# An attention and feed-forward kernel: head pairs taken two at a time on TensorE, PSUM pools laid out anew behind the opening, and the order of every engine written out

## The chip, the cores and the metric

The kernel runs on one core of a Trainium2 chip. Five engines work beside each other, each through its own instructions in order: TensorE (PE in the profile; PEld is its weight load), VectorE (DVE), ScalarE (ACT), GpSimd (POOL) and SyncE (SP), whose queue issues all loads and stores here. The metric is the device time of one execution in microseconds; lower is better.

## The reference

Queries, keys and values have 4 batches x 8 heads x 768 positions x 64. Each query sees the keys less than 16 positions away, and 24 summaries of blocks of 32 keys (the maximum of the keys, the mean of the values, with log 32 added to the score). The result is laid side by side by heads (512 columns) and goes through a feed-forward layer with 2048 hidden columns.

```python
k_sum = k.reshape(B, H, nb, block, D).max(axis=3)      # block 32
v_sum = v.reshape(B, H, nb, block, D).mean(axis=3)
scores_l = where(|i - j| < 16, scale * q @ k.T, -1e9)
scores_s = scale * q @ k_sum.T + log(block)
a = softmax(concatenate([scores_l, scores_s]))         # + 1e-9 under the fraction
x = a @ concatenate([v, v_sum])                        # heads side by side: 3072 x 512
h = x @ w_in
g = where(h >= 1, h, where(h <= -1, 0, (h + 1) ** 2 / 4))
out = g @ w_out
```

## The kernel before

The 3072 tokens are cut into eight chunks of 384 (half a batch each). A chunk's attention runs over four pairs of heads; a pair's two heads (j = 0, 1) lie in the two halves of the partitions. 384 queries are six blocks of 64, and each block sees a window of 96 keys and the 24 summaries: 120 columns.

Every step has a letter, and behind it the chunk, then the pair, hidden tile or part. For a pair: k, q, v load (k[c,p] is the windows, 360 KB; q 384 KB, half of it zeros, since the two heads' queries stand in their own columns of a block of 128), and r, y load the raw keys and values at the first chunk of a batch; R takes the maxima of the keys and C spreads them behind the windows; S makes the scores (12 matmuls in float32, L247, which the profile counts as 24); M masks them and takes the row maxima; E, D, N are the exponentials, the reciprocals of their sums and the product of both; t turns the result with 12 transposes of 32x32 blocks on VectorE (L300; T and P do so on TensorE and ScalarE in chunks 0 and 1); Y, z and x make the value means and spread them behind the windows of values; A multiplies with the values (again 12 matmuls, counted as 24, L310); X and L split the result into a high and a low part (xhi, xlo).

The feed-forward part goes through 16 hidden tiles of 128 per chunk. F (L331) is the first layer: four parts of three matmuls into one PSUM bank h, of which there are two (the pool ps_h). G and H (ACT), I (DVE, the last to read h; L350), J (ACT) and O (POOL, L360) make the activation and split it. B (L369) is the second layer: nine matmuls into the three banks acc of the chunk, two hidden tiles behind F (LAG = 2). U copies acc out and o stores it.

PSUM has the two banks of ps_h and six of the pool ps, which scores, turned weights, values and acc share. Up to the first F steps of chunk 1 the order of every engine is written out (OPENING, under tc.manual_schedule()). From there on the program lists, for each hidden tile, F, G, H, I, J, O, then one quarter of a pair's attention of the next chunk (a generator, attention), then B; Tile's scheduler orders each engine's instructions from that by its own costs. One pair therefore takes four hidden tiles, and TensorE makes eight short visits a chunk between F and B: four of scores, four of values.

The softmax weights of a pair lie in one tile e of two buffers, the turned weights in one tile turned_blocks for both heads of a pair. Raw keys, raw values and outputs share three buffers (tag "w" of the pool stage); keys, values and queries have two each.

## Time and profile before

| | |
|---|---|
| time, median of three runs | 666.75 us (664.21 to 668.29) |
| the profiled execution | 664.14 us |
| its span, first to last instruction | 662.4 us |
| granted TensorE clock, mean | 0.992 |
| TensorE busy | 638.6 us, 96% |
| VectorE, ScalarE, GpSimd busy | 57%, 53%, 45% |
| DMA | 69.07 MB, mean 104 GB/s |

The profile shows one execution. A busy time sums what an engine executed; matmuls overlap, and their ends are modelled. In the timeline a row has the start, the duration, the engine, the line, the operation, what it writes and reads, its shape and how often; in brackets the idle time before it and what released the engine. Neighbours of one kind are merged into one row (x24). In a row of stages stand the stage, its length, busy time and count of PE, PEld, DVE, ACT and POOL (or of those that match), the granted clock, the DMA share and GB/s. Times in the trace count from its first instruction.

### The profile page before, as it was taken

To read this page: it belongs to the slowest core of one execution; us is meant where nothing else is said; L and a number is where in the kernel's file an instruction comes from. 1 tells how busy PE (TensorE), PEld (TensorE's weight loads), DVE (VectorE), ACT (ScalarE), POOL (GpSimd) and SP (SyncE) were. 2 spreads that over 40 slices of the span, in tenths; PEclk is the share of its full clock that TensorE was granted. 3 is DMA by queue.
4 is the path that set the end of the run, shared out by engine and by line. 5 is a ranking of instruction groups with operands and counts; after the bars stand their busy time and mean duration, and the time that the engine had idled before them with its cause. 6 is when DMAs were issued, how large, how long until landed. Compare 5 with 4: busy or idle time off the path is not lost.

```text
span 662.4 us, 11908 instructions
## 1 busy us (share of the span) xinstructions
PE 638.6 (96%) x4442; PEld 559.9 (85%) x4442; DVE 376.8 (57%) x897; ACT 348.7 (53%) x881; POOL 295.2 (45%) x296
## 2 busy tenths in 40 slices
PE   8789997879999999999899999999999999999997
PEld 8679896758888888888788888888888888889996
DVE  5999974668445745557554755449645654431111
ACT  3899965644544454544544554554444545444332
POOL 2669985544444444225444433425444334222221
PEclk9999999898999999999999999999999999999999
DMA  8999502842222412145211411127102210001001
GB/s 293 325 355 332 216 1 103 284 156 65 66 65 65 135 44 66 46 133 186 66 52 32 160 50 62 64 81 239 56 29 65 99 60 19 2 1 47 1 0 48
DMA packets 31401, 69.07 MB, mean 104 GB/s; under 512 B 2928, under 2 KB 11376, under 8 KB 31344
## 3 DMA queue, kind: packets, MB, share of 16 engines
...
q14 instruction: 22, 0.18, 0.1%
...
## 4 chain that ended last, share of the span: by engine, by line
PE 78%; DVE 10%; DMA 5%; ACT 3%; issue 2%; POOL 1%; SPq 0%; POOLq 0%; DVEq 0%; ACTq 0%
PE acc L369 37%; PE h L331 35%; PE o_ps L310 3%; PE s_ps L247 3%; DMA first<-in_kT 2%; ACT e L267 2%; DVE turned_blocks L300 1%; DMA vraw<-in_vT 1%; DVE e L257 1%; DVE t L350 1%; DVE den L262 1%; DVE c L124 1%; DVE den L272 1%; DVE sums L213 1%; POOL e L277 1%
## 5 line engine op out<-in xcount | busy, mean ns | idle before, releaser
L331 PE MATMUL h<-xhi,halves 128*128 128x384 f32 x1024 | 284.8, 340 | 2.0 <-DVE t L350 2.0
L360 POOL TENSOR_TENSOR glo<-t,ghi 128x384 fp32r<-128x384 f32 x128 | 129.7, 1015 | 279.0 <-ACT ghi L355 185.7
L369 PE MATMUL acc<-halves,ghi 128*128 128x512 f32 x768 | 240.7, 394 | 0.0
L331 PEld LDWEIGHTS h<-xhi,halves 128*128 128x128 f32 x1024 | 188.5, 189 | 8.5 <-issue 2.1
L350 DVE SCALAR_TENSOR_TENSOR t<-h,t 128x384 f32<-128x384 f32 x128 | 70.9, 556 | 187.0 <-ACT t L347 178.6
L331 PE MATMUL h<-xlo,halves 128*128 128x384 f32 x512 | 173.9, 340 | 0.0
L369 PEld LDWEIGHTS acc<-halves,ghi 128*128 128x128 f32 x768 | 144.7, 188 | 28.8
L369 PE MATMUL acc<-halves,glo 128*128 128x512 f32 x384 | 156.7, 408 | 1.5 <-POOL glo L360 1.5
L355 ACT CAST ghi<-t 128x384 fp32r<-128x384 f32 x128 | 65.4, 513 | 150.0 <-DVE t L350 149.9
L344 ACT ACTIVATE t<-h,ones_half 128x384 f32<-128x384 f32 x128 | 73.7, 576 | 107.2 <-PE h L331 105.5
L300 DVE STREAM_TRANSPOSE turned_blocks<-e 32x192 f32<-32x192 f32 x288 | 106.5, 370 | 30.1 <-POOL e L277 25.7
L331 PEld LDWEIGHTS h<-xlo,halves 128*128 128x128 f32 x512 | 96.6, 189 | 5.7 <-DVE xlo L321 0.2
L267 ACT ACTIVATE e<-e,den 128x120 f32<-128x120 f32 x192 | 73.3, 383 | 28.3 <-DVE den L262 28.2
L369 PEld LDWEIGHTS acc<-halves,glo 128*128 128x128 f32 x384 | 72.1, 188 | 18.5 <-issue 3.6
L347 ACT ACTIVATE t<-t 128x384 f32<-128x384 f32 x128 | 67.1, 525 | 4.0
L277 POOL TENSOR_TENSOR e<-e,den 128x360 f32<-128x360 f32 x64 | 50.4, 790 | 40.6 <-DVE den L273 22.7
L222 POOL TENSOR_SCALAR v<-means 32x768 f32<-32x768 f32 x24 | 51.1, 2128 | 5.1 <-DVE means L219 1.6
L143 POOL TENSOR_TENSOR halves<-w,halves 128x1024 fp32r<-128x1024 f32 x16 | 38.5, 2417 | 3.4 <-ACT halves L137 2.8
L272 DVE TENSOR_SCALAR den<-den 128x3 f32<-128x3 f32 x64 | 16.4, 257 | 35.5 <-ACT e L267 35.4
L267 ACT ACTIVATION_READ_ACCUMULATOR e<-e,den 128x1 f32 x192 | 35.9, 187 | 0.0
L257 DVE SCALAR_TENSOR_TENSOR e<-s_ps,mask_sb 128x360 f32<-128x360 f32 x64 | 30.8, 523 | 1.8 <-PE s_ps L247 1.8
L262 DVE TENSOR_REDUCE den<-e 128x3 f32<-128x360 f32 x64 | 30.5, 518 | 0.0
...
## 6 DMA issues: line engine op xcount, KB each, us to landing
q<-in_q SPq DMA_DIRECT2D x30, 384.0 KB, 4.2
...
raw<-in_w_in SPq DMA_DIRECT2D x16, 512.0 KB, 10.5
raw<-in_w_out SPq DMA_DIRECT2D x16, 512.0 KB, 10.7
...
kraw<-in_kT SPq DMA_DIRECT2D x13, 384.0 KB, 4.0
vraw<-in_vT SPq DMA_DIRECT2D x13, 384.0 KB, 4.0
```

What stands on the lines that cost most here:

```text
L143: nc.gpsimd.tensor_tensor(out=lo, in0=converting[i].bitcast(F32), in1=hi.bitcast(F32), op=ALU.subtract)
L222: nc.gpsimd.tensor_scalar(out=v_ts[c, p][KW:], in0=means[p * SB:(p + 1) * SB].unsqueeze(1).broadcast_to([SB, NB, P]), scalar1=1.0 / SB, sc ...
L267: nc.scalar.activation(out=e[:, t, :], in_=e[:, t, :], func=AF.Exp, bias=nm[:, t:t + 1], scale=1.0, accum_out=den[:, t:t + 1])
L277: nc.gpsimd.tensor_tensor(out=e, in0=e, in1=den.unsqueeze(2).broadcast_to([P, NT, KA]), op=ALU.mult)
L300: nc.vector.transpose(out=pt[kb * SB:(kb + 1) * SB, :, qb * SB:(qb + 1) * SB], in_=e[qb * SB:(qb + 1) * SB, :, at:at + SB])
L331: nc.tensor.matmul(hs[c, f][:, :T], weight["win", f][w][:, k * P:(k + 1) * P], x, start=(k == 0 and n == 0), stop=(k == NK - 1 and n == 2))
L344: nc.scalar.activation(out=ts[c, f], in_=hs[c, f][:, :T], func=AF.Relu, bias=ones_half, scale=0.5)
L347: nc.scalar.square(out=ts[c, f], in_=ts[c, f])
L350: nc.vector.scalar_tensor_tensor(out=ts[c, f], in0=hs[c, f][:, :T], scalar=1.0, in1=ts[c, f], op0=ALU.max, op1=ALU.min)
L355: nc.scalar.copy(out=hi, in_=ts[c, f])
L360: nc.gpsimd.tensor_tensor(out=lo, in0=ts[c, f], in1=hi.bitcast(F32), op=ALU.subtract)
L369: nc.tensor.matmul(acc[c][i], a[:, rows], weight["wout", f][w], start=(f == 0 and n == 0), stop=(f == NF - 1 and n == 2))
```

## The change

It leaves the opening's order and the arithmetic as they are, with these edits behind and around it:

- Steps s and p take the scores and the values of two pairs (h = 0 or 1) in one go: 24 matmuls, counted as 48. The four banks for s are one of ps_h and three of a new pool ps_att, which p shares; acc has a new pool ps_acc of three banks. Both, and a new att_later, are opened where ps and att are closed behind the opening.
- Masks (n) are single steps; maxima (i), reciprocals (h) and products (l) take both heads of a pair in one instruction; each exponential (g) and each row of transposes (t) is a step. e holds two pairs in one buffer, turned_blocks two pairs.
- The value means are scaled on VectorE (u) ahead of their transposes, and x is a copy instead of a product.
- From chunk 1 on queries are loaded without zeros, by two DMAs of half the partitions; chunk 0's first two pairs of queries go to a room of the weights, as the other two did.
- SECOND (the feed-forward part of chunk 1) and LATER (chunks 2 to 7, and the end) write out the order of everything behind the opening. A sign stands for the chunk: "." the chunk whose feed-forward part runs, "-" the one before, "+" the next and "*" the one after that. Steps that were done are skipped.

In this diff a line of "..." stands where lines are left out.

```diff
 """
+SECOND = """
+v+0 v+1 F.00 F.01 F.02 F.03 r+0 k+0 q+0 r+1 G.0 k+1 q+1 H.0 I.0 R+0 J.0 F.10 F.11 F.12 F.13 O.0 R+1 C+0 G.1 C+1 y+0
+y+1 H.1 I.1 J.1 F.20 F.21 F.22 F.23 U-1 O.1 o-1 u+0 s+0 G.2 H.2 u+1 U-0 k+2 U-2 o-0 n+00 B.0 o-2 I.2 q+2 n+01 J.2 n+10
+k+3 n+11 q+3 i+0 F.30 F.31 F.32 F.33 O.2 i+1 r+2 g+00 r+3 g+01 z+0 g+02 z+1 B.1 G.3 x+0 g+03 x+1 H.3 g+04 I.3 g+05
+F.40 F.41 F.42 F.43 R+2 J.3 g+10 O.3 h+0 g+11 R+3 g+12 l+0 g+13 B.2 y+2 G.4 y+3 g+14 C+2 t+00 H.4 C+3 g+15 t+01 F.50
+F.51 F.52 F.53 I.4 h+1 J.4 l+1 t+02 B.3 G.5 O.4 t+03 H.5 I.5 J.5 F.60 F.61 F.62 F.63 t+10 O.5 t+11 B.4 G.6 t+12 H.6
+t+13 I.6 J.6 F.70 F.71 F.72 F.73 u+2 O.6 u+3 p+0 G.7 H.7 z+2 I.7 X+0 v+2 B.5 X+1 v+3 z+3 J.7 L+0 L+1 F.80 F.81 F.82
+F.83 O.7 x+2 B.6 G.8 x+3 H.8 I.8 J.8 F.90 F.91 F.92 F.93 O.8 s+1 G.9 H.9 I.9 r*0 B.7 n+20 J.9 k*0 n+21 q*0 n+30 n+31
+r*1 i+2 F.a0 F.a1 F.a2 F.a3 O.9 k*1 q*1 i+3 g+20 g+21 R*0 g+22 B.8 G.a C*0 g+23 H.a R*1 g+24 g+25 I.a C*1 y*0 F.b0
+F.b1 F.b2 F.b3 g+30 h+2 y*1 J.a l+2 g+31 g+32 g+33 B.9 O.a t+20 G.b g+34 t+21 H.b g+35 I.b F.c0 F.c1 F.c2 F.c3 h+3 J.b
+l+3 t+22 t+23 B.a G.c O.b H.c t+30 I.c t+31 F.d0 F.d1 F.d2 F.d3 J.c O.c t+32 t+33 B.b G.d H.d u*0 F.e0 F.e1 F.e2 F.e3
+I.d z*0 J.d u*1 O.d p+1 G.e H.e z*1 I.e X+2 v*0 B.c X+3 v*1 L+2 J.e L+3 F.f0 F.f1 F.f2 F.f3 O.e x*0 B.d G.f x*1 H.f
+I.f J.f
+"""
+LATER = """
+F.00 F.01 F.02 F.03 O-f s+0 G.0 H.0 I.0 k+2 B-e n+00 J.0 q+2 n+01 n+10 k+3 n+11 q+3 i+0 F.10 F.11 F.12 F.13 O.0 i+1
+g+00 g+01 g+02 B-f G.1 g+03 H.1 g+04 I.1 g+05 F.20 F.21 F.22 F.23 U-1 U-0 h+0 U-2 o-1 l+0 J.1 o-0 g+10 o-2 g+11 B.0
+G.2 O.1 t+00 g+12 t+01 H.2 r+2 g+13 r+3 F.30 F.31 F.32 F.33 I.2 g+14 g+15 t+02 J.2 h+1 O.2 t+03 B.1 G.3 l+1 H.3 R+2
+I.3 F.40 F.41 F.42 F.43 C+2 t+10 J.3 t+11 O.3 B.2 G.4 t+12 H.4 t+13 I.4 J.4 F.50 F.51 F.52 F.53 O.4 R+3 C+3 y+2 B.3
+G.5 y+3 H.5 I.5 J.5 F.60 F.61 F.62 F.63 O.5 u+2 p+0 G.6 u+3 H.6 I.6 X+0 v+2 B.4 z+2 X+1 v+3 J.6 L+0 L+1 z+3 F.70 F.71
+F.72 F.73 O.6 x+2 B.5 G.7 x+3 H.7 I.7 J.7 F.80 F.81 F.82 F.83 O.7 s+1 G.8 H.8 I.8 r*0 B.6 n+20 J.8 k*0 n+21 q*0 n+30
+n+31 r*1 i+2 F.90 F.91 F.92 F.93 O.8 k*1 q*1 i+3 g+20 g+21 R*0 g+22 B.7 G.9 C*0 g+23 H.9 R*1 g+24 g+25 I.9 C*1 y*0
+F.a0 F.a1 F.a2 F.a3 g+30 h+2 y*1 J.9 l+2 g+31 g+32 g+33 B.8 O.9 t+20 G.a g+34 t+21 H.a g+35 I.a F.b0 F.b1 F.b2 F.b3
+h+3 J.a l+3 t+22 t+23 B.9 G.b O.a H.b t+30 I.b t+31 F.c0 F.c1 F.c2 F.c3 J.b O.b t+32 t+33 B.a G.c H.c u*0 F.d0 F.d1
+F.d2 F.d3 I.c z*0 J.c u*1 O.c B.b G.d H.d z*1 I.d F.e0 F.e1 F.e2 F.e3 J.d O.d p+1 G.e H.e I.e X+2 v*0 B.c X+3 v*1 L+2
+J.e L+3 F.f0 F.f1 F.f2 F.f3 O.e x*0 B.d G.f x*1 H.f I.f J.f
+"""
 FIRST = [[("k", 2), ("q", 2)], [("k", 3), ("q", 3)], [("kraw", 1), ("vraw", 1)], [("kraw", 2), ("vraw", 2)],
-         [("kraw", 3), ("vraw", 3)], [("v", 2), ("v", 3)]]
+         [("kraw", 3), ("vraw", 3)], [("v", 2), ("v", 3)],
+         [("q", 0), ("q", 1)]]
 K_COPY = "vgvg"
 HI_POOL = [0, 2, 4, 6, 8, 10, 12, 14]
 
...
     load = ctx.enter_context(tc.tile_pool(name="load", bufs=2))
     ps_h = ctx.enter_context(tc.tile_pool(name="ps_h", bufs=2, space=PSUM))
-    ps = ctx.enter_context(tc.tile_pool(name="ps", bufs=6, space=PSUM))
+    opening = ExitStack()
+    ps = opening.enter_context(tc.tile_pool(name="ps", bufs=6, space=PSUM))
+    att = opening.enter_context(tc.tile_pool(name="att", bufs=2))
...
     def load_queries(c, p):
         b, hf = divmod(c, NHALF)
-        q_ts[c, p] = input_tile(load, "q", [P, NB, P], c, p)
-        nc.sync.dma_start(out=q_ts[c, p], in_=q2[b, p, :, hf * NB:(hf + 1) * NB, :])
+        blocks = slice(hf * NB, (hf + 1) * NB)
+        q_ts[c, p] = input_tile(load, "q", [P, NB, QB], c, p)
+        if c == 0:
+            nc.sync.dma_start(out=q_ts[c, p], in_=q2[b, p, :, blocks, :])
+        else:
+            for j in range(2):
+                rows = slice(j * D, (j + 1) * D)
+                nc.sync.dma_start(out=q_ts[c, p][rows], in_=q2[b, p, rows, blocks, rows])
...
+    def sum_vals_ahead(c, p):
+        part = sums[:, p, SB - NSUM:]
+        nc.vector.tensor_reduce(out=part, in_=raws["v", p].rearrange("p (n j) -> p n j", j=SB), axis=AX.X, op=ALU.add)
+        nc.vector.tensor_scalar_mul(out=part, in0=part, scalar1=1.0 / SB)
...
     def spread_sums(c, p):
-        nc.gpsimd.tensor_scalar(out=v_ts[c, p][KW:], in0=means[p * SB:(p + 1) * SB].unsqueeze(1).broadcast_to([SB, NB, P]),
-                                scalar1=1.0 / SB, scalar2=None, op0=ALU.mult)
+        nc.gpsimd.tensor_copy(out=v_ts[c, p][KW:], in_=means[p * SB:(p + 1) * SB].unsqueeze(1).broadcast_to([SB, NB, P]))
...
+    def scores_of_two(c, h):
+        for n in range(2 * NT):
+            b, t = divmod(n, NT)
+            p = 2 * h + b
+            if t == 0:
+                for j in range(2):
+                    where, tag = (ps_h, "h") if (b, j) == (0, 0) else (ps_att, "att")
+                    s_pss[c, p, j] = where.tile([P, 512], F32, tag=tag, name=f"s_ps{c}_{p}_{j}")
+            q_t, k_t = q_ts[c, p], k_ts[c, p]
+            for j in range(2):
+                rows = slice(j * D, (j + 1) * D)
+                for i in range(2):
+                    nc.tensor.matmul(s_pss[c, p, j][i * QB:(i + 1) * QB, t * KA:(t + 1) * KA], q_t[rows, 2 * t + i],
+                                     k_t[rows, 2 * t + i], start=True, stop=True)
+    def mask_of(c, p, j):
+        h, b = divmod(p, 2)
+        if (c, h) not in es:
+            es[c, h] = att.tile([P, 2, 2, NT, KA], F32, tag="e", name=f"e{c}_{h}", bufs=1)
+        at = c % NHALF
+        nc.vector.scalar_tensor_tensor(
+            out=es[c, h][:, b, j], in0=s_pss[c, p, j][:, :NT * KA].rearrange("p (t n) -> p t n", n=KA), scalar=1.0 / math.sqrt(D),
+            in1=mask_sb[:, at:at + NT], op0=ALU.mult, op1=ALU.add)
+    def maxima(c, p):
+        h, b = divmod(p, 2)
+        dens[c, p] = att.tile([P, 2, 2, NT], F32, tag=f"den{b}", name=f"den{c}_{p}")
+        nc.vector.tensor_reduce(out=dens[c, p][:, 0].rearrange("p j t -> p (j t)"), in_=es[c, h][:, b].rearrange("p j t k -> p (j t) k"), axis=AX.X, op=ALU.max, negate=True)
+    def exp_of(c, p, u):
+        h, b = divmod(p, 2)
+        j, t = divmod(u, NT)
+        e = es[c, h][:, b, j, t, :]
+        nc.scalar.activation(out=e, in_=e, func=AF.Exp, bias=dens[c, p][:, 0, j, t:t + 1], scale=1.0,
+                             accum_out=dens[c, p][:, 1, j, t:t + 1])
+    def reciprocals_of_pair(c, p):
+        den = dens[c, p][:, 1].rearrange("p j t -> p (j t)")
+        nc.vector.tensor_scalar_add(out=den, in0=den, scalar1=1e-9)
+        nc.vector.reciprocal(out=den, in_=den)
+    def norms_of_pair(c, p):
+        h, b = divmod(p, 2)
+        e = es[c, h][:, b].rearrange("p j t k -> p (j t) k")
+        den = dens[c, p][:, 1].rearrange("p j t -> p (j t)")
+        nc.gpsimd.tensor_tensor(out=e, in0=e, in1=den.unsqueeze(2).broadcast_to([P, 2 * NT, KA]), op=ALU.mult)
+    def turn_blocks(c, p, kb):
+        h, b = divmod(p, 2)
+        e = es[c, h][:, b].rearrange("p j t k -> p (j t) k")
+        pt = turned_blocks[:, b]
+        at = min(kb * SB, KA - SB)
+        for qb in range(P // SB):
+            if kb == P // SB - 1 or kb - qb % 2 in (0, 1):
+                nc.vector.transpose(out=pt[kb * SB:(kb + 1) * SB, :, qb * SB:(qb + 1) * SB],
+                                    in_=e[qb * SB:(qb + 1) * SB, :, at:at + SB])
+    def values_of_two(c, h):
+        for b in range(2):
+            p = 2 * h + b
+            o_pss[c, p] = ps_att.tile([P, 512], F32, tag="att", name=f"o_ps{c}_{p}")
+            for blk in range(NB):
+                t, i = divmod(blk, 2)
+                for j in range(2):
+                    nc.tensor.matmul(o_pss[c, p][j * D:(j + 1) * D, blk * QB:(blk + 1) * QB], v_ts[c, p][:, blk, j * D:(j + 1) * D],
+                                     turned_blocks[:, b, j * NT + t, i * QB:(i + 1) * QB], start=True, stop=True)
...
-            acc[c] = [ps.tile([P, DM], F32, tag="ps", name=f"acc{c}_{i}") for i in range(NTT)]
+            acc[c] = [(ps if c == 0 else ps_acc).tile([P, DM], F32, tag="ps", name=f"acc{c}_{i}") for i in range(NTT)]
...
+    def at_chunk(text, c):
+        for step in text.split():
+            at = c + "-.+*".index(step[1]) - 1
+            if at < NCH and not (step[0] in "rRyuz" and at % NHALF):
+                do(step[0] + str(at) + step[2:])
...
     with tc.manual_schedule():
         do(OPENING)
-    turned_on_vector.update(range(NHALF, NCH))
-    turned_blocks = att.tile([P, 2, T], F32, tag="pt", name="turned_blocks", bufs=1)
-    for j in range(2):
-        nc.gpsimd.memset(turned_blocks[:, j], 0.0)
-    sums = const.tile([P, NPAIR, SB], F32, name="sums")
-    means = const.tile([P, P], F32, name="means")
-    nc.gpsimd.memset(sums, 0.0)
-
-    ahead = {c: attention(c) for c in range(1, NCH)}
-    for i in range(NF, NCH * NF + LAG):
-        c, f = divmod(i, NF)
-        if i < NCH * NF:
-            s = f"{c}{f:x}"
-            do(f"F{s}0 F{s}1 F{s}2 F{s}3 G{s} H{s} I{s} J{s} O{s}")
-            if c + 1 < NCH:
-                next(ahead[c + 1])
-        c, f = divmod(i - LAG, NF)
-        do(f"B{c}{f:x}")
-        if f == NF - 1:
-            do(" ".join(f"U{c}{i} o{c}{i}" for i in range(NTT)))
+        opening.close()
+        att = ctx.enter_context(tc.tile_pool(name="att_later", bufs=2))
+        ps_acc = ctx.enter_context(tc.tile_pool(name="ps_acc", bufs=NTT, space=PSUM))
+        ps_att = ctx.enter_context(tc.tile_pool(name="ps_att", bufs=3, space=PSUM))
+        turned_blocks = att.tile([P, 2, 2 * NT, P], F32, tag="turned", name="turned_blocks", bufs=1)
+        for b in range(2):
+            nc.gpsimd.memset(turned_blocks[:, b], 0.0)
+        sums = const.tile([P, NPAIR, SB], F32, name="sums")
+        means = const.tile([P, P], F32, name="means")
+        nc.gpsimd.memset(sums, 0.0)
+        at_chunk(SECOND, 1)
+        for c in range(2, NCH + 1):
+            at_chunk(LATER, c)
```

More of the change, by code (lines that the diff above doesn't have):

```diff
@@ L218, in turn_sums @@
             rows = slice(a * SB, (a + 1) * SB)
-            nc.vector.transpose(out=means[p * SB:(p + 1) * SB, rows], in_=sums[rows, p, :])
+            nc.vector.transpose(out=means[p * SB:(p + 1) * SB, rows], in_=sums[rows, p])
     def spread_sums(c, p):
-        nc.gpsimd.tensor_scalar(out=v_ts[c, p][KW:], in0=means[p * SB:(p + 1) * SB].unsqueeze(1).broadcast_to([SB, NB, P]),
-                                scalar1=1.0 / SB, scalar2=None, op0=ALU.mult)
+        nc.gpsimd.tensor_copy(out=v_ts[c, p][KW:], in_=means[p * SB:(p + 1) * SB].unsqueeze(1).broadcast_to([SB, NB, P]))
     def turn_vals(c, p):
@@ L247, in scores @@
                     nc.tensor.matmul(s_ps[j][i * QB:(i + 1) * QB, t * KA:(t + 1) * KA],
-                                     q_t[rows, blk, rows], k_t[rows, blk, :], start=True, stop=True)
+                                     q_t[rows, blk, rows] if c == 0 else q_t[rows, blk], k_t[rows, blk, :], start=True, stop=True)
         s_pss[c, p] = s_ps
@@ L284, in turned @@
     def turned(c, p, j):
-        if (c, p) not in pts:
-            pts[c, p] = att.tile([P, 2, T], F32, tag="pt", name=f"pt{c}_{p}", bufs=1)
-        pts[c, p, j] = pts[c, p][:, j]
+        pts[c, p, j] = att.tile([P, T], F32, tag=f"pt{j}", name=f"pt{c}_{p}_{j}", bufs=1)
         nc.scalar.copy(out=pts[c, p, j][:KA], in_=t_pss[c, p, j][:KA, :T])
-    def turn_blocks(c, p):
-        pts[c, p] = turned_blocks
-        e = es[c, p].rearrange("p j t k -> p (j t) k")
-        pt = pts[c, p].rearrange("p j (t q) -> p (j t) q", q=P)
-        for kb in range(P // SB):
-            at = min(kb * SB, KA - SB)
-            for qb in range(P // SB):
-                if kb == 3 or kb - qb % 2 in (0, 1):
-                    nc.vector.transpose(out=pt[kb * SB:(kb + 1) * SB, :, qb * SB:(qb + 1) * SB],
-                                        in_=e[qb * SB:(qb + 1) * SB, :, at:at + SB])
-        for j in range(2):
-            pts[c, p, j] = pts[c, p][:, j]
     def values(c, p):
@@ L309, in values @@
             for j in range(2):
-                nc.tensor.matmul(o_pss[c, p][j * D:(j + 1) * D, cols], v_ts[c, p][:keys_of(c), blk, j * D:(j + 1) * D],
-                                 pts[c, p, j][:keys_of(c), cols], start=True, stop=True)
+                nc.tensor.matmul(o_pss[c, p][j * D:(j + 1) * D, cols], v_ts[c, p][:KA, blk, j * D:(j + 1) * D],
+                                 pts[c, p, j][:KA, cols], start=True, stop=True)
     def high(c, p):
@@ L393, in fused_kernel @@
         "K": window_keys, "R": sum_keys, "C": summary_keys, "S": scores, "M": masks, "E": exps, "D": reciprocals, "N": norms,
-        "T": transposes, "P": turned, "Y": sum_vals, "Z": turn_vals, "V": mean_vals, "W": spread_vals, "A": values, "X": high, "L": low,
+        "T": transposes, "P": turned, "Y": sum_vals, "Z": turn_vals, "V": mean_vals, "W": spread_vals, "A": values, "X": high,
+        "s": scores_of_two, "n": mask_of, "i": maxima, "g": exp_of, "h": reciprocals_of_pair, "l": norms_of_pair, "t": turn_blocks,
+        "p": values_of_two, "u": sum_vals_ahead, "z": turn_sums, "x": spread_sums, "L": low,
         "a": convert_top, "b": convert_low, "c": convert_join, "d": convert_high, "e": convert_rest,
-        "F": ff1, "G": gate_half, "H": gate_square, "I": gate_min, "J": gate_high, "O": gate_rest, "B": ff2, "t": turn_blocks, "z": turn_sums, "x": spread_sums, "U": result, "o": store, "j": idle_products,
+        "F": ff1, "G": gate_half, "H": gate_square, "I": gate_min, "J": gate_high, "O": gate_rest, "B": ff2, "U": result, "o": store, "j": idle_products,
     }
@@ L404, in do @@
                 steps[step[0]](*(int(x, 16) for x in step[1:]))
-    def attention(c):
-        first = c % NHALF == 0
-        for p in range(NPAIR):
-            s = f"{c}{p}"
-            do((f"r{s} " if first else "") + f"k{s} q{s} " + (f"R{s} " if first else "") + f"C{s} S{s} M{s}")
-            for j in range(2):
-                do(f"E{s}{j} D{s}{j} N{s}{j}")
-            yield
-            if c in turned_on_vector:
-                do((f"y{s} " if first else "") + f"v{s} " + (f"Y{s} z{s} " if first else "") + f"x{s}")
-                yield
-                do(f"t{s}")
-                yield
-            else:
-                do((f"y{s} " if first else "") + f"v{s} " + (f"Y{s} " if first else "") + f"Z{s} V{s} W{s}")
-                yield
-                do(f"T{s}0 P{s}0 T{s}1 P{s}1")
-                yield
-            do(f"A{s} X{s} L{s}")
-            yield
@@ L429, in fused_kernel @@
-    turned_on_vector = set()
+    def at_chunk(text, c):
[3 more added lines that the diff above has]
+                do(step[0] + str(at) + step[2:])
     with tc.manual_schedule():
         do(OPENING)
-    turned_on_vector.update(range(NHALF, NCH))
-    turned_blocks = att.tile([P, 2, T], F32, tag="pt", name="turned_blocks", bufs=1)
-    for j in range(2):
-        nc.gpsimd.memset(turned_blocks[:, j], 0.0)
```

12 lines of the change are left out of this document (3 added, 9 removed).

## The prediction

> **What bounds the kernel now.** I read the page's busy times first, then busy times by stage, then single stretches of TensorE's timeline.
>
> ```profile
> PE 638.6 (96%) x4442; PEld 559.9 (85%) x4442; DVE 376.8 (57%) x897; ACT 348.7 (53%) x881; POOL 295.2 (45%) x296
> 130.91:153.84 22.93, 18.45 (x145) 15.45 (x141) 16.19 (x39) 9.84 (x28) 10.26 (x13) 0.93 0.43 136
> 153.84:584.92 431.08, 429.07 (x2996) 375.51 (x2992) 245.32 (x630) 211.72 (x582) 180.21 (x180) 1.00 0.24 76
> ```
>
> TensorE is the bound: from 153.84 to 584.92 us it stands still for 2 us in 431, while DVE, ACT and POOL are busy for 57%, 49% and 42% of it. So from there on only what TensorE executes, and its few gaps, can change the time; a faster ACT or POOL is worth nothing. The 23 us ahead of it, where chunk 1 begins its feed-forward part and chunk 2 its attention, are another matter (DVE 16 of 23 us, a granted clock of 0.93).
>
> **What a visit costs.** Two stretches of TensorE's timeline, with a scores visit between the two layers and without one:
>
> ```profile
> 400.13 0.34 PE L331 MATMUL h<-xhi,halves 128*128 128x384 f32 x1
> 400.40 0.85 PE L247 MATMUL s_ps<-k,q 64*64 64x120 f32 x24
> 401.18 0.50 PE L369 MATMUL acc<-halves,glo 128*128 128x512 f32 x1
> 401.52 0.39 PE L369 MATMUL acc<-halves,ghi 128*128 128x512 f32 x1
> ...
> 405.31 0.34 PE L331 MATMUL h<-xhi,halves 128*128 128x384 f32 x1
> 405.49 0.39 PE L369 MATMUL acc<-halves,glo 128*128 128x512 f32 x1
> 405.72 0.39 PE L369 MATMUL acc<-halves,ghi 128*128 128x512 f32 x1
> ```
>
> From the last h to the first acc it is 1.05 us with the visit and 0.18 without; the next acc then follows after 0.34 instead of 0.23. A scores visit costs 0.87 + 0.11 = 0.98 us. A values visit, and what a second set of 24 adds:
>
> ```profile
> 166.38 0.34 PE L331 MATMUL h<-xhi,halves 128*128 128x384 f32 x1
> 166.65 0.92 PE L310 MATMUL o_ps<-turned_blocks,v 128*64 128x64 f32 x24
> 167.50 0.50 PE L369 MATMUL acc<-halves,glo 128*128 128x512 f32 x1
> 167.83 0.62 PE L369 MATMUL acc<-halves,ghi 128*128 128x512 f32 x2
> ...
> 109.24 1.58 PE L247 MATMUL s_ps<-k,q 64*64 64x120 f32 x48
> 110.75 0.68 PE L227 MATMUL vs_ps<-ident_sb,vs 128*24 128x128 f32 x4
> ...
> 148.71 0.80 PE L310 MATMUL o_ps<-turned_blocks,v 128*64 128x64 f32 x20
> ```
>
> Values: 1.12 - 0.18 + 0.10 = 1.04 us. The opening has two scores visits back to back: 48 matmuls take 1.51 us from their start to the next, 24 take 0.78, so the second 24 add 0.73, and joining saves 0.98 - 0.73 = 0.25. For values, 24 take 0.12 longer than 20, so 24 more add 0.72, and joining saves 1.04 - 0.72 = 0.32. Chunks 2 to 7 have four of each now and two of each after: 12 joins of scores, 12 of values, 3.0 + 3.8 = **6.8 us**. Ends: 0 if the visit breaks in its middle, 7.7 if scores join as well as values; I take the rows.
>
> **The late gaps.** They are these, on TensorE:
>
> ```profile
> 316.02 0.44 PE L331 MATMUL h<-xhi,halves 128*128 128x384 f32 x1 [0.65 <-DVE t L350]
> 319.15 0.34 PE L310 MATMUL o_ps<-turned_blocks,v 128*64 128x64 f32 x4 [0.75 <-PE h L331]
> 319.89 0.80 PE L310 MATMUL o_ps<-turned_blocks,v 128*64 128x64 f32 x20 [0.41 <-DVE turned_blocks L300]
> 471.07 0.80 PE L310 MATMUL o_ps<-turned_blocks,v 128*64 128x64 f32 x20 [0.20 <-DVE turned_blocks L300]
> ```
>
> All hang on DVE's transposes ending as their values visit comes up. In the new order of chunk 2 and later the last turned block stands two feed-forward steps (some 8 us) ahead of its values visit: t+13 is ahead of I.4 and p+0 behind F.6, t+33 ahead of I.c and p+1 behind F.e (in chunk 1's order one step). The four sum to **2.0 us**, which I take as gone (end: 0).
>
> **The transition, 130.91 to 153.84.** Work in it at plain prices:
>
> ```profile
> 130.91:153.84 22.93, 11.70 (x51) 0.93 0.43 136
> 130.91:153.84 22.93, 4.61 (x18) 0.93 0.43 136
> 156.20 2.11 PE h L331 x12
> 158.30 2.09 PE acc L369 x9
> 142.62 0.50 PE L369 MATMUL acc<-halves,glo 128*128 128x512 f32 x1 [1.45 <-POOL glo L360]
> 147.97 0.34 PE L310 MATMUL o_ps<-turned_blocks,v 128*64 128x64 f32 x4 [2.99 <-issue]
> ```
>
> The first two rows count first-layer and second-layer matmuls: 51/12 x 2.11 + 18/9 x 2.09 + one values visit 1.04 + two scores visits 1.96 = 16.15 us; 6.8 us are lost, 4.4 of them in the two gaps and the rest at a halved clock. What the new order does here:
>
> ```profile
> 131.06 0.33 SPq L191 DMA_DIRECT2D v<-in_vwin  x1
> 131.50 0.37 SPq L167 DMA_DIRECT2D kraw<-in_kT  x1
> q<-in_q SPq DMA_DIRECT2D x30, 384.0 KB, 4.2
> raw<-in_w_in SPq DMA_DIRECT2D x16, 512.0 KB, 10.5
> kraw<-in_kT SPq DMA_DIRECT2D x13, 384.0 KB, 4.0
> L205 DVE TENSOR_REDUCE ks<-kraw 128x24 f32<-128x768 f32 x13 | 12.3, 950 | 0.8 <-DMA kraw<-in_kT 0.6
> 401.81 0.56 DVE L350 SCALAR_TENSOR_TENSOR t<-h,t 128x384 f32<-128x384 f32 x1 [4.23 <-ACT t L347]
> 134.46 0.96 DVE L257 SCALAR_TENSOR_TENSOR e<-s_ps,mask_sb 128x360 f32<-128x360 f32 x2
> ```
>
> SP's queue begins with v+0 and v+1, and v+1 waits, as now, for the last values visit of chunk 1 (131.06); behind it stand r+0 (131.5), k+0, two issues of q+0, then r+1 at about 133.1 (0.4 us each). r+1 lands 4.0 us later, behind three transfers rather 4.7: 137.1 to 137.8. DVE's order is I.0, R+0, R+1, I.1, so R+1 (0.95) and then I.1 (0.56) end at 138.6 to 139.3; say 139.0. The visit s+0 lies behind F.2 and takes one of the two h banks, that of h.1, which only I.1 frees. TensorE gets there at 130.91 + 30 matmuls x 0.176 + 0.3 of waiting for I.0 = 136.5, and waits 2.5. Then s+0 (1.7) and B.0 (2.1) end at 142.8. F.3 needs I.2, and DVE has u+0, u+1 and n+00 ahead of it: y+1 is issued when R+0 has freed its buffer (136.5), lands at 140.5, u+1 ends at 141.7, n+00 (0.48) and I.2 (0.56) at 142.8 or up to 0.7 later; 0.5 lost. Together 0.3 + 2.5 + 0.5 = 3.3.
>
> Does 2.5 us of standstill halve the clock?
>
> ```profile
> 142.62:146.31 3.69, 2.36 (x9) 1.62 (x9) 2.63 (x7) 1.51 (x3) 1.94 (x3) 1.00 0.00 0
> 149.72:153.13 3.41, 3.41 (x15) 2.97 (x18) 3.32 (x8) 0.46 (x2) 1.59 (x2) 0.51 0.26 87
> ```
>
> The gap of 1.45 us was followed by a clock of 1.00, the one of 2.99 by 3.41 us at 0.51, which costs 1.7. 2.5 lies between, nearer to the second; half of such a price may fall on the wait for I.2, so I add 0.9 (ends 0 and 1.7). By the Trainium skill ("TensorE: Matmul & The Clock Gate", Part 1: an idle window of about 3.4 us halves the clock) a gap of 2.5 us need not do it, and the sum would be 0.9 lower; the trace shows that 2.99 did, so the rule is not met to the letter here.
>
> So 4.2 is lost instead of 6.8: 2.6 gained. Ahead of it, DVE no longer mixes chunk 2's key sums into chunk 1's attention:
>
> ```profile
> 120.41 0.94 DVE L205 TENSOR_REDUCE ks<-kraw 128x24 f32<-128x768 f32 x1
> L377 ACT COPY o<-acc 128x512 f32<-128x512 f32 x16 | 9.1, 577 | 7.0 <-PE acc L369 7.0
> ```
>
> The first row's 0.94 stands ahead of pair 3's mask, on the chain to chunk 1's last values visit; I take 0.8 (ends 0 and 0.94). The transition gives **3.4 us** (ends -2 and 6.8).
>
> **What I cost at nothing.** Halved queries: the bytes fall, the pieces shrink to 256 bytes and each load becomes two issues; from chunk 2's second pair of pairs on they are asked for seven steps (30 us) ahead, so only the transition feels them. Spreading the value means as a copy, scaling on DVE, one reduce, reciprocal and norm per pair instead of two: all on engines at half load. The h bank lent to the scores: from the last h (400.47) the evacuation ends with DVE's L350 at 402.37, 1.9 us, beneath a joined visit and a second-layer step (1.7 + 2.1); spare 1.9. Three acc banks for two chunks: the copies (0.58 each) lie beneath F.2 (2.11); uncovered, 6 x 0.58 = 3.5 us. The last chunk's tail is unchanged.
>
> **Sum.** 6.8 + 2.0 + 3.4 = 12.2 us. The profiled execution took 664.14 (span 662.4 and 1.7 around it) and would take 651.9. The median of the runs, 666.75, is 2.6 above it; carried over: **654.6**.
>
> **Rivals.**
> - *The queue at the transition eats its gain* (0.12). The page counts whole loads alone, so a load in 256-byte pieces has no row: from below 4.2 us (the present q load, twice the bytes), from above 10.5 (the weight load, in 1 KB pieces, behind others). I took the lower, as the nearest in kind. At 10.5, q+1 (issued by 134.5) lands at 145, s+0's second half waits some 5 us more, and the time is 659.6. Against it: bytes are halved. The Trainium skill ("DMA: Bandwidth & Descriptors", Specifications) asks for at least 512 bytes a piece for full rate, which speaks for this rival; no row here shows pieces of 256 bytes.
> - *The joined visit breaks in two* (0.07): pair 1's first matmuls wait for their own keys, banks or blocks, and the switching stays. Then 6.8 is not gained: 661.4. Against it: the x48 row, which ran through.
> - *The lent h bank comes back late* (0.05), the slower end. For the length of a scores visit one h bank is left, so the next first-layer step waits for I. One run of DVE's transposes ahead of I decides, as now:
>
> ```profile
> 467.94 3.08 DVE L300 STREAM_TRANSPOSE turned_blocks<-e 32x192 f32<-32x192 f32 x8
> ```
>
> A lateness over the spare 1.9 us is lost at each of 12 visits. From 3.5 us on (12 x 1.6 = 19, the gain and 1% more) the kernel is slower; a whole pair's 12 transposes (12 x 0.385 = 4.6) cost 12 x 2.7 = 32 us: 687. The written order has no transposes between s and I. By the Trainium skill ("Perfetto Trace Analysis", Matmuls) independent groups should rotate through PSUM banks so that evacuation overlaps the next group, which is what the lent bank gives up.
>
> **The numbers.** The forecast has 0.70; its own range is 648.5 to 659 (7.7 for joining and 6.8 at the transition below; the gaps kept, half the clock and no gain ahead above). The rivals have 0.24, and 0.06 is for small new waits in a wholly new order, half within 1%, half slower. This kernel's runs differ by some 0.6%, so 1% (660.1 and 673.4) is about what can be told from none. Faster: 0.70 of the forecast less 0.01, and 0.08 of the first rival: 0.77. Same: 0.01 + 0.04 + 0.07 + 0.03 = 0.15. Slower: 0.08. The range 648.5 to 661.5 takes in the forecast, the first rival and about half of the second.
>
> **What would show it.** After: joined visits of 48 with 1.5 us from start to the next for scores, 1.5 to 1.6 for values; 16 steps and four visits a chunk with no TensorE gap from about 150 us on; one gap of 2 to 3 us ahead of the first s+0, put down to DVE's L350, and perhaps one stretch of 3.4 us at half clock behind it. TensorE's last matmul comes 12 us earlier. Wrong, if gaps of over 0.5 us recur in every chunk (the third rival), if a visit of 48 shows a gap in its middle (the second), or if s+0's wait is for q (the first).

## The result, and the profile after

The changed kernel takes 656.02 us (median of 4 runs, 655.24 to 656.93) where the kernel before, run beside it, takes 665.48 (664.08 to 668.29): a ratio of 0.9853, with a 95% interval of 0.9813 to 0.9893. The forecast was 654.6, in a range of 648.5 to 661.5. The profiled execution took 656.5 us, 654.5 of it span, against 664.14 and 662.4 before: 7.9 us of span, where the sum of the terms was 12.2. The direction came out, and most of the size; this part shows which terms did not.

First the page of the changed kernel, the busy times and the loads of queries and raw keys:

```profile
PE 630.8 (96%) x4442; PEld 561.3 (86%) x4442; DVE 372.3 (57%) x837; ACT 345.1 (53%) x881; POOL 259.4 (40%) x272
...
q<-in_q SPq DMA_DIRECT2D x56, 96.0 KB, 4.2
kraw<-in_kT SPq DMA_DIRECT2D x13, 384.0 KB, 4.6
```

TensorE still executes 4442 matmuls and is busy for 7.8 us less. Then its busy time by stage (stage, length, busy time and count of PE, PEld, DVE, ACT and POOL, granted clock, DMA share, GB/s), changed kernel:

```profile
132.58:167.71 35.13, 31.42 (x208) 27.59 (x208) 23.23 (x56) 15.05 (x45) 13.11 (x17) 0.95 0.56 165
172.00:645.00 473.00, 473.00 (x3236) 423.50 (x3235) 241.67 (x570) 228.63 (x610) 159.28 (x168) 1.00 0.20 61
```

From 172 to 645 us TensorE has not one gap: 473.00 of 473.00. All that is left to lose behind the opening lies in the first row, the transition, where it stands still for 3.7 us and has a clock of 0.95. A joined visit of each kind on TensorE's timeline, with the step behind it, and for the second the evacuation on VectorE (step I) that frees the one h bank left beside the lent one, on which the next h waits:

```profile
167.44 0.34 PE L421 MATMUL h<-xhi,halves 128*128 128x384 f32 x1
167.71 1.62 PE L410 MATMUL o_ps<-turned_blocks,v 128*64 128x64 f32 x48
169.25 0.50 PE L459 MATMUL acc<-halves,glo 128*128 128x512 f32 x1
...
177.60 0.34 PE L421 MATMUL h<-xhi,halves 128*128 128x384 f32 x1
177.87 1.46 PE L355 MATMUL s_ps<-k,q 64*64 64x120 f32 x48
179.26 0.50 PE L459 MATMUL acc<-halves,glo 128*128 128x512 f32 x1
...
179.27 0.56 DVE L440 SCALAR_TENSOR_TENSOR t<-h,t 128x384 f32<-128x384 f32 x1 [3.64 <-ACT t L437]
...
181.45 0.34 PE L421 MATMUL h<-xhi,halves 128*128 128x384 f32 x1
```

From its start to the next matmul a joined scores visit takes 1.39 us and a joined values visit 1.54, without a break inside. Two single visits took 2 x 0.78 and 2 x 0.85, and paid the 0.1 us ahead of and the 0.1 us behind a visit twice: a join saves 0.37 and 0.36.

The transition, TensorE first, from the last values visit of chunk 1 on:

```profile
132.58 1.54 PE L327 MATMUL o_ps<-pt,v 120*64 120x64 f32 x24 [0.57 <-ACT pt L320]
134.06 0.69 PE L421 MATMUL h<-xhi,halves 128*128 128x384 f32 x1
...
143.51 1.60 PE L355 MATMUL s_ps<-k,q 64*64 64x120 f32 x48 [2.56 <-DVE t L440]
...
147.95 0.44 PE L421 MATMUL h<-xhi,halves 128*128 128x384 f32 x1 [0.55 <-DVE e L363]
```

SyncE's queue in the same stretch:

```profile
121.59 12.94 SPq L222 DMA_DIRECT2D v<-in_vwin  x4
134.58 0.42 SPq L196 DMA_DIRECT2D kraw<-in_kT  x1
...
135.52 1.28 SPq L213 DMA_DIRECT2D q<-in_q  x2
136.84 0.61 SPq L196 DMA_DIRECT2D kraw<-in_kT  x1
```

and VectorE:

```profile
138.43 0.94 DVE L236 TENSOR_REDUCE ks<-kraw 128x24 f32<-128x768 f32 x1
141.99 0.95 DVE L236 TENSOR_REDUCE ks<-kraw 128x24 f32<-128x768 f32 x1 [2.62 <-DMA kraw<-in_kT]
142.86 0.55 DVE L440 SCALAR_TENSOR_TENSOR t<-h,t 128x384 f32<-128x384 f32 x1
```

The forecast gap is there, 2.56 us ahead of s+0, and put down to the L440 that was named. But the row above it is what counts, R+1, which waits for the raw keys. SP's queue holds these back. Its row x4 merges four issues of v, of 0.3 us each, at 121.59, 125.57, 130.62 and 134.21; the time between them is waiting. The last two are v+0 and v+1: each stands at the queue's head until a values visit of chunk 1 has read its buffer, for 4.6 and 3.2 us. So the raw keys behind them leave only at 134.58 and 136.84.

Last, the end, as the timeline shows it: the last matmuls and SP's stores, before

```profile
657.95 1.71 SPq L381 DMA_DIRECT2D out<-o  x3
...
658.06 0.62 PE L369 MATMUL acc<-halves,ghi 128*128 128x512 f32 x2
```

and after, with the copies of acc:

```profile
648.60 0.59 ACT L467 COPY o<-acc 128x512 f32<-128x512 f32 x1 [2.47 <-PE acc L459]
649.29 0.69 DVE L465 COPY o<-acc 128x512 f32<-128x512 f32 x1 [3.71 <-PE acc L459]
...
650.01 1.30 SPq L471 DMA_DIRECT2D out<-o  x3
```

TensorE ends at 658.68 and at 649.94; the span goes on for 3.7 us before and for 4.6 after. The first store used to be issued while the last matmuls ran, and is now issued behind them: o-1 stands ahead of o-0 in the order and waits for VectorE's copy (649.98), while ScalarE's copy has been there since 649.19.

The span's 7.9 us by stretches, from the starts of the first second-layer matmul, of the first scores visit of 48 and of chunk 1's last values visit, and TensorE's end (before 47.99, 109.24, 130.06, 658.68; after 50.02, 111.69, 132.58, 649.94): up to the first 2.0 longer, then 0.4 and 0.1 longer, then 528.62 against 517.36, 11.3 shorter, and the tail 0.9 longer.

### The profile page after: what moved, and what is told of

It is laid out like the page before. It is cut to its first block, busy times and chain, and to the rows that moved or that the text cites. A ratio compares the mean times of both kernels' runs of the same rounds, so it can differ in the third digit from the quotient of the medians.

```text
span 654.5 us, 11884 instructions
## 1 busy us (share of the span) xinstructions
PE 630.8 (96%) x4442; PEld 561.3 (86%) x4442; DVE 372.3 (57%) x837; ACT 345.1 (53%) x881; POOL 259.4 (40%) x272
## 4 chain that ended last, share of the span: by engine, by line
PE 85%; DVE 4%; DMA 4%; POOL 2%; ACT 2%; issue 2%; SPq 1%; POOLq 0%; ACTq 0%; DVEq 0%
PE acc L459 39%; PE h L421 37%; PE o_ps L410 3%; DMA first<-in_kT 3%; PE s_ps L355 2%; PE o_ps L327 1%; DMA vraw<-in_vT 1%; PE t_ps L316 1%; POOL glo L450 1%; DVE turned_blocks L400 1%; ACT e L301 1%; POOL halves L172 1%; PE h_idle L429 1%; DVE w L159 0%; PE s_ps L283 0%
## 5 line engine op out<-in xcount | busy, mean ns | idle before, releaser
L440 DVE SCALAR_TENSOR_TENSOR t<-h,t 128x384 f32<-128x384 f32 x128 | 71.2, 557 | 215.1 <-ACT t L437 204.7
L459 PE MATMUL acc<-halves,glo 128*128 128x512 f32 x384 | 154.6, 402 | 0.4 <-POOL glo L450 0.4
L388 POOL TENSOR_TENSOR e<-e,den 128x720 f32<-128x720 f32 x24 | 33.4, 1391 | 48.7 <-DVE den L382 25.5
L376 ACT ACTIVATION_READ_ACCUMULATOR e<-e,den 128x1 f32 x144 | 27.5, 191 | 0.0
L429 PE MATMUL h_idle<-zeros 128*128 128x128 f32 x162 | 23.4, 304 | 1.0 <-POOL zeros L112 1.0
L429 PEld LDWEIGHTS h_idle<-zeros 128*128 128x128 f32 x162 | 21.8, 216 | 1.6 <-POOL zeros L112 1.0
L363 DVE SCALAR_TENSOR_TENSOR e<-s_ps,mask_sb 128x360 f32<-128x360 f32 x48 | 22.2, 524 | 0.0
```

The source lines that it names most:

```text
L376: nc.scalar.activation(out=e, in_=e, func=AF.Exp, bias=dens[c, p][:, 0, j, t:t + 1], scale=1.0, accum_out=dens[c, p][:, 1, j, t:t + 1])
L388: nc.gpsimd.tensor_tensor(out=e, in0=e, in1=den.unsqueeze(2).broadcast_to([P, 2 * NT, KA]), op=ALU.mult)
L429: nc.tensor.matmul(hs["idle"][:, :P], zeros, zeros, start=True, stop=True)
L440: nc.vector.scalar_tensor_tensor(out=ts[c, f], in0=hs[c, f][:, :T], scalar=1.0, in1=ts[c, f], op0=ALU.max, op1=ALU.min)
L459: nc.tensor.matmul(acc[c][i], a[:, rows], weight["wout", f][w], start=(f == 0 and n == 0), stop=(f == NF - 1 and n == 2))
```

## The experiments

The theory: the gain is the joined visits, which save the change between the large matmuls of the feed-forward part and the small ones of attention; the transition gave little because SP's queue holds the raw keys back. Rivals: the gain is the written order and the gaps it closes; the transition is limited by the halved queries; with one h bank lent, the other costs something everywhere.

**Joins undone.**

```diff
 # in scores_of_two and values_of_two, behind the first pair's matmuls
+ff2(*pending[0], [0])        # the first three of the next B's nine matmuls
 # B then does the six that are left
```

> The changed kernel, but each joined visit (12 of scores, 12 of values) is broken in its middle by three of the nine second-layer matmuls that follow it anyway; same matmuls, same work elsewhere. If the price of a visit is the switch in and out (the forecast's 0.25 for scores and 0.32 for values), the time rises by 6.8 us, or by up to 8.5 if both cost some 0.35. If the gain of the change came from its order and not from joining, the time stays within 1 us.

Measured: 664.85 us (663.25 to 666.78), a ratio to the kernel before of 0.9991 (0.9972 to 1.0010). It is 8.8 us above the changed kernel: nothing of the gain is left. A broken values visit in its timeline:

```profile
313.57 0.92 PE L412 MATMUL o_ps<-turned_blocks,v 128*64 128x64 f32 x24
314.42 0.50 PE L469 MATMUL acc<-halves,glo 128*128 128x512 f32 x1
...
315.31 0.92 PE L412 MATMUL o_ps<-turned_blocks,v 128*64 128x64 f32 x24
316.16 0.50 PE L469 MATMUL acc<-halves,glo 128*128 128x512 f32 x1
```

The two halves take 0.85 each, and the three matmuls between them 0.89 instead of 0.70. From the first joined values visit behind the transition to the last acc row it is 489.67 us here and 481.61 in the changed kernel: 8.06 for 23 joins, 0.35 each. The Trainium skill ("TensorEngine Tiling (Array Packing)", Key Properties) says that a change of the tiling mode drains TensorE, and gives no price. The runs fit that, and the price of a visit, there and back, is 0.35 us here. TensorE has no gap in this kernel either (478.00 us busy of the 478.00 from 172 to 650), so the price lies in the spacing of the matmuls and not in a gap that the profile shows. The two kinds of matmul differ in their tile and in their type (float32 in attention, float32r in the feed-forward part); no run shows which of the two makes the price.

**Keys ahead of values in SP's queue.**

```diff
-v+0 v+1 F.00 F.01 F.02 F.03 r+0 k+0 q+0 r+1 G.0 k+1 q+1 H.0 I.0 ...
+r+0 k+0 r+1 k+1 q+0 q+1 v+0 v+1 F.00 F.01 F.02 F.03 G.0 H.0 I.0 ...
```

> The changed kernel with one edit in the order of chunk 1: the raw keys, keys and queries of the first two pairs stand ahead of the two value loads in SP's queue. If the gap of 2.56 us ahead of the first joined scores visit comes from SP's queue standing at the second value load, it goes, and with it the 0.55 behind: 3 us less. If the gap comes from how long the key loads take once issued, or from the halved clock, the time stays within 1 us.

Measured: 651.91 us (649.93 to 655.7), ratio 0.9796 (0.9754 to 0.9838), 4.1 less than the changed kernel by the medians; the runs spread widely, and the slowest is as slow as the changed kernel's. SP's queue and TensorE's stage from chunk 1's last values visit to the first joined one:

```profile
124.95 0.42 SPq L196 DMA_DIRECT2D kraw<-in_kT  x1
...
125.90 0.42 SPq L196 DMA_DIRECT2D kraw<-in_kT  x1
```

```profile
131.62:161.19 29.57, 29.32 (x207) 26.08 (x207) 23.16 (x56) 15.06 (x45) 13.03 (x17) 1.00 0.56 149
```

The raw keys leave 6.7 and 5.7 us ahead of that values visit's start, not 2.0 and 4.3 behind it. The stage that took 35.13 us takes 29.57, with 0.25 us of standstill and a clock of 1.00: in this trace the whole loss of the transition is gone. That the queue made the gap, and not VectorE's order or the lent bank, is shown: only loads changed their places, and in all four traces with this order the gap is gone. The clock is another matter: in the three kernels below that have this order too, and queries without zeros, the stage takes 31.3 to 31.6 us, without a gap over 0.3 us but with a stretch at half clock.

**Queries in one piece of 1,536 bytes a partition**, packed on the way in, for chunks 1 to 7.

```diff
-            for j in range(2):
-                rows = slice(j * D, (j + 1) * D)
-                nc.sync.dma_start(out=q_ts[c, p][rows], in_=q2[b, p, rows, blocks, rows])
+            nc.sync.dma_start(out=q_ts[c, p], in_=q3[b, p, :, blocks, :])
```

> The changed kernel with the queries of chunks 1 to 7 laid out without zeros beforehand, so that a load is one DMA of 1,536-byte pieces and not two of 256-byte pieces. If the pieces' size is hidden but for the transition (forecast), the time falls by 0 to 1 us. If pieces of 256 bytes cost as the rule on 512 bytes has it, the transition's loads land earlier and the time falls by 2 us or more.

Measured: 655.52 us (652.28 to 656.89), ratio 0.9837 (0.9803 to 0.9871), 0.5 below the changed kernel, which its spread covers. From the first joined values visit to the last acc row it is 481.60 us, against 481.61: behind the transition the pieces of 256 bytes are hidden. In the transition, where one issue takes the place of two, this trace shows 33.30 us for the stage that took 35.13; of that the medians show 0.5 at most. Its first joined scores visit waits for 1.38 us instead of 2.56, but TensorE runs at half clock up to 139.46 us, 5.6 us from chunk 1's last values visit on, and so comes to that visit later. The Trainium skill ("DMA: Bandwidth & Descriptors", Specifications) asks for 512 bytes a piece for full rate; behind the transition, with loads asked for 30 us ahead, the smaller pieces cost no engine anything here.

**The kernel before, once more**, to see how far its opening varies.

> The kernel before, unchanged, for a second trace. In the changed kernel's trace the second layer begins at 50.0 us, in that of before at 48.0. If the opening's 2 us are the change's, this trace shows 48.0 within 0.5; if they are how loads happen to fall in a run, it may show any value between 48 and 50.

Measured: 663.82 us (one run), and its second layer begins at 48.37 us (47.99 in the first profile).

**The other h bank, held longer**: copies on VectorE ahead of the I that frees the h bank left beside the lent one, at each of the 12 joined scores visits; they compute nothing that is used.

```diff
+    for _ in range(5):                     # 13 in the second kernel
+        nc.vector.tensor_copy(out=spare, in_=ts[c, f])
     # ahead of the first I behind each s
```

> The changed kernel with five extra copies of 128x384 on VectorE ahead of step I in each of the twelve hidden tiles whose scores visit has one h bank lent (some 0.34 us each by the row of such copies, 1.7 together; their output is read by nobody). The forecast gives the lent bank 1.9 us to spare: if so, no change beyond 1 us in the stretch behind 170 us, and no TensorE gap in front of the first-layer step that follows. If the spare is not there, each of the twelve visits loses up to 1.7: 20 us.

> The same with thirteen copies, some 4.4 us. With 1.9 to spare each of the twelve visits loses some 2.5 us: 30 us, more where the clock is halved behind such a gap (1.7 each, up to 20). If a late bank is hidden in some other way, under 5 us.

Measured: 662.59 us with 5 copies and 724.46 with 13, one run each. With 5, a visit in the timeline, VectorE and then TensorE:

```profile
178.87 1.94 DVE L501 COPY spare<-t 128x384 f32<-128x384 f32 x5 [3.58 <-ACT t L437]
180.92 0.56 DVE L440 SCALAR_TENSOR_TENSOR t<-h,t 128x384 f32<-128x384 f32 x1
...
181.53 0.44 PE L421 MATMUL h<-xhi,halves 128*128 128x384 f32 x1 [0.24 <-DVE t L440]
```

In the changed kernel I ends 1.96 us behind the visit's start; here the visit starts at 177.53 and I ends at 181.48, so it is 2.0 late, and the next h starts 0.42 late. So the spare is 1.6 us: in the changed kernel I ends at 179.83 and the h that needs the bank starts at 181.45. Over the stretch from the first joined values visit, 488.05 us against 481.61, each of 11 visits loses 0.59. With 13 copies, one visit in the timeline, and then the stage behind its gap:

```profile
307.15 1.46 PE L355 MATMUL s_ps<-k,q 64*64 64x120 f32 x48
308.49 5.10 DVE L501 COPY spare<-t 128x384 f32<-128x384 f32 x13 [3.57 <-ACT t L437]
...
314.30 0.69 PE L421 MATMUL h<-xhi,halves 128*128 128x384 f32 x1 [3.40 <-DVE t L440]
```

```profile
314.30:317.70 3.40, 3.40 (x11) 3.40 (x12) 3.33 (x6) 1.34 (x6) 1.01 (x1) 0.50 0.01 2
317.70:321.00 3.30, 3.30 (x12) 2.79 (x11) 0.92 (x2) 2.79 (x12) 0.00 (x0) 0.69 0.00 0
```

The standstill of 3.40 us is followed by half the clock for the whole of the first stage and some 2.0 us of the second, 5.4 us together. From chunk 1's last values visit to TensorE's end it is 585.65 us against 517.36: 5.7 us a visit, of which 3.5 is the lateness over the spare (5.1 of copies less 1.6); the other 2.2 are of the size of the halved clock, whose 5.4 us cost 2.7 at this visit. So the third rival had its mechanism right and its price too low: 12 x 5.7 = 68 us. It did not decide because nothing in the written order stands between s and I.

**All queries packed, chunk 0's too**, with the keys ahead. Chunk 0's first two pairs of queries in the weights' room, then in the load pool.

```diff
-            shape = {"q": [NB, P], ...
+            shape = {"q": [NB, QB], ...
-        if c == 0:  ... two forms of load
+        nc.sync.dma_start(out=q_ts[c, p], in_=q3[b, p, :, blocks, :])
 # the second kernel only:
-         [("kraw", 3), ("vraw", 3)], [("v", 2), ("v", 3)],
-         [("q", 0), ("q", 1)]]
+         [("kraw", 3), ("vraw", 3)], [("v", 2), ("v", 3)]]
```

> The changed kernel with the keys ahead of the values in chunk 1's order, and all queries, chunk 0's too, laid out without zeros beforehand and loaded by one DMA each. The opening's DMA engines are busy throughout its first 50 us, and chunk 0's queries are 0.79 MB less at about 0.34 MB per us: if the opening hangs on bytes, 2.3 us less than the keys-first kernel (651.9 to about 649.5). If it hangs on the conversion of the weights or on how loads fall, within 1 us of it.

> The same, with chunk 0's first two pairs of queries in the pool of queries again and not in a room of the weights. The second layer began at 48.0 and 48.4 us in two traces of before and at 49.0 to 51.4 in four with the room: if the room is why, it begins some 1.7 us earlier here than in the kernel with the room; if not, at the same time.

Measured: 648.46 us (646.93 to 650.44), ratio 0.9727 (0.9698 to 0.9757), and 649.81 (648.06 to 650.07), ratio 0.9745 (0.9727 to 0.9763). The second layer begins at 47.08 and 47.65 us. The room makes no difference that can be told, so the queries' new place is not why the changed kernel's opening is later; with fewer bytes to load the opening is sooner (47.98 in the last kernel below). The busy times of one stretch of the opening, in the kernel before, in the changed one and in the first of these two:

```profile
30.00:40.00 10.00, 7.88 (x113) 7.04 (x114) 9.90 (x21) 8.95 (x14) 4.61 (x7) 1.00 1.06 323
```

```profile
30.00:40.00 10.00, 8.06 (x90) 7.23 (x90) 9.86 (x20) 7.77 (x15) 5.09 (x7) 0.83 1.06 302
```

```profile
30.00:40.00 10.00, 8.78 (x118) 7.95 (x119) 9.93 (x20) 8.48 (x15) 3.90 (x7) 1.00 1.06 333
```

The DMA engines are full in all three (1.06); what differs is what they moved, 323, 302 and 333 GB/s, and in the changed kernel half of the clock for 3.4 us. That stretch alone is not why: the second of these two has it in its opening too (a clock of 0.83 from 30 to 40 us). With whole queries in chunk 0 the changed kernel and its variants began the second layer between 48.35 and 51.41 us in eight traces, the kernel before at 47.99 and 48.37 in two. Why the opening is later, by 1.4 us on the average, is open.

**The order of the last stores.**

```diff
-... U-1 U-0 h+0 U-2 o-1 l+0 J.1 o-0 g+10 o-2 ...
+... U-1 U-0 h+0 U-2 o-0 l+0 J.1 o-1 g+10 o-2 ...
```

> The changed kernel with the stores of a chunk's three results in the order 0, 1, 2 on SP's queue instead of 1, 0, 2. Its last chunk ends 4.56 us behind the last second-layer matmul's record, against 3.68 before, because the first store stands behind the copy of result 1. If that order is why: 0.9 us off that tail in the trace and off the time. If the tail hangs on the last store alone, which comes at the same moment either way: no change.

Measured: 655.5 us (654.53 to 657.67), ratio 0.9845 (0.9820 to 0.9870). Its timeline ends so, SP and TensorE:

```profile
648.46 1.71 SPq L471 DMA_DIRECT2D out<-o  x3
...
648.57 0.62 PE L459 MATMUL acc<-halves,ghi 128*128 128x512 f32 x2
```

The store is issued ahead of the last matmuls' end again, and the tail takes 3.9 us instead of 4.6. The 0.5 us between the medians is of that size, but the spread of the runs covers it; the order is shown by the trace alone.

**The value means scaled by the copy's engine again**, on POOL as before the change.

```diff
-        nc.vector.tensor_scalar_mul(out=part, in0=part, scalar1=1.0 / SB)
...
-        nc.gpsimd.tensor_copy(out=v_ts[c, p][KW:], in_=means...)
+        nc.gpsimd.tensor_scalar(out=v_ts[c, p][KW:], in0=means..., scalar1=1.0 / SB, scalar2=None, op0=ALU.mult)
```

> The changed kernel with the value means spread by a product on GpSimd again (2.1 us each instead of 0.86) and without the scaling on VectorE. Forecast: GpSimd is far from the bound and nothing behind these rows is late, so the time stays within 1 us. If GpSimd's queue is what holds the order together, a gap shows at the values visits and the time rises by 2 us or more.

Measured: 657.78 us (656.23 to 662.91), ratio 0.9886 (0.9848 to 0.9925). On TensorE, the first joined scores visit, the first joined values visit and the last acc row:

```profile
141.58 2.85 PE L355 MATMUL s_ps<-k,q 64*64 64x120 f32 x48 [3.79 <-DVE t L440]
...
167.29 1.62 PE L410 MATMUL o_ps<-turned_blocks,v 128*64 128x64 f32 x48
...
648.91 0.62 PE L459 MATMUL acc<-halves,ghi 128*128 128x512 f32 x2
```

From the values visit to the last acc row it is 481.62 us, as in the changed kernel: behind the transition the product on POOL costs nothing, and so the copy in its place gains nothing. What this kernel has more lies in the transition, and its cause isn't the product. The kernel with broken visits, which has the copy, shows the same there:

```profile
130.44 0.92 PE L327 MATMUL o_ps<-pt,v 120*64 120x64 f32 x24 [0.68 <-ACT pt L320]
...
141.23 1.59 PE L355 MATMUL s_ps<-k,q 64*64 64x120 f32 x24 [3.88 <-DVE t L444]
```

```profile
141.40:146.00 4.60, 4.60 (x52) 3.25 (x52) 2.75 (x6) 1.27 (x3) 1.23 (x2) 0.50 0.65 197
```

So the same order of loads goes at least two ways. Where chunk 1's last values visit runs at half clock (1.48 us in the changed kernel), the gap is 2.6 us and full clock follows; where it runs at full clock (0.85 here), TensorE is there sooner, stands still for 3.3 to 3.9 us, and then runs at half clock. The stage to the first joined values visit takes 34.8 and 35.1 us the one way and 36.0 to 36.6 the other (36.4 with the product, 130.88 to 167.29). The kernel with 13 copies, the first of which come behind this visit, had both: the half clock ahead, a gap of 2.42 us, 0.85 more inside the visit, where 20 of its 48 matmuls waited for a load of queries, and half the clock again behind it.

**Together**: keys ahead, all queries packed, stores in order.

> Keys ahead of values in chunk 1's order, all queries without zeros by one DMA each, stores in the order 0, 1, 2. The first two gave 648.5; with the tail's 0.9 some 647.6, if the parts add. If the loads of a run drown it, 648 to 650.

Measured: 648.38 us (647.41 to 649.89), ratio 0.9729 (0.9703 to 0.9756): 2.7% under the kernel before and some 7.6 us under the changed one. It is the best of these kernels together with the one without the stores' order (648.46), from which it can't be told apart.

## Why the prediction was right, and where not

**The bound.** Right: TensorE sets the time, and from 172 us on it has no gap.

**Joins, 6.8 us.** The mechanism was right and the size too low: 0.25 for scores and 0.32 for values were forecast, and the rows show 0.37 and 0.36, the broken visits 0.35 on the average; 24 make 8.4 us, and 8.8 by the medians. The term that was off is the scores' "second 24 add 0.73", from one visit of 48 in the opening: 48 now take 1.39 us, not 1.51, so that row held some 0.1 us that was not the matmuls' own. For the values 24 more add 0.69, where 0.72 was forecast. The upper end, 7.7, gave both the values' 0.32 and was too low as well.

**Late gaps, 2.0 us.** Right: there are none behind 172 us.

**The transition, 3.4 us.** This step failed. The loss there was to fall from 6.8 to 4.2 us. With the keys ahead the stage from chunk 1's last values visit to the first joined one takes 29.57 us, 29.3 without its standstill; the changed kernel's 35.13 thus lose 5.8, and 1.0 was gained instead of 2.6; the variants with the longer gap, at 36.0 to 36.6 us, gained next to nothing. Of the 5.8, standstill is 3.7 (forecast 3.3) and the rest 2.1 (forecast 0.9), so the halved clock is the term that was most out. "SP's queue begins with v+0 and v+1, and v+1 waits, as now, for the last values visit" was right, and so was the chain behind it, r+1, R+1, I.1, s+0. Its terms too were small. The two issues of q+0 take 1.28 us, not 0.8, so r+1 leaves 2.8 us behind the visit's end (136.84 against 134.06), where 2.2 was forecast; and R+1 starts 5.15 us behind that issue, where 4.0 to 4.7 was. I.1 therefore ends 9.4 us behind the visit, not 8.1. That the gap came out at 2.56 (forecast 2.5) is chance: TensorE was late as well, at half clock up to about 135.9, by as much as the keys. The forecast let the half clock come behind the gap, at half its price (0.9); in every trace with this order at least 3.2 us at half clock are paid (3.35 here, which cost 1.7), ahead of the gap or behind it.

The 0.8 ahead of the transition was not gained: from the first scores visit of 48 to chunk 1's last values visit it is 20.82 us before and 20.89 after. VectorE's key sum is gone from it, but did not set its end; what does is not shown.

From chunk 1's last values visit to TensorE's end that is 8.4 + 2.0 + 1.0 = 11.4, against 11.3 measured.

**At nothing.** Behind the transition the halved queries, the value means and the three acc banks cost nothing, as said. The spare of the h bank left is 1.6 us instead of 1.9, since the step that needs the bank comes 0.3 us sooner than it was put; nothing came near it. "The last chunk's tail is unchanged" was wrong by 0.9 us: the stores' order in LATER was not read through to the end, where nothing is behind it to hide it.

**What was not in the sum.** The opening, 2.0 us later in the profiled execution and 0.4 more up to the first scores visit of 48, for a reason that stays open.

**The sum.** 12.2 was forecast and 7.6 came, between the profiled executions: joins 1.6 more, transition 2.5 less, opening 2.4 less, tail 0.9 less, which leaves 0.4 for what lies around the span and for rounding. Between the medians it is 9.5, since the profiled execution of before lay 1.3 below the median of the runs beside it, and that of after 0.5 above. So part of the opening's 2 us may be a difference of two executions rather than of two kernels; no run settles it. That the forecast came within 1.4 us is in good part luck: the joins made up for more than half of what the transition did not give, and the forecast stood on a median of 666.75 us for the kernel before, which beside the changed one ran at 665.48, 1.3 less.

**The rivals.** The first had a part in it, mainly by another cause than the size of the pieces: with the keys ahead in the queue the stage of the transition is 5.6 us shorter in one trace and 3.5 to 3.9 in three. Its sign, a wait of s+0 for q, came in one trace, that of the kernel with 13 copies (0.85 us). The second and the third did not occur in the changed kernel; brought about by the two edits above, they cost 8.8 and 68 us.
